# Seven block products in place of eight in the last tile of a windowed attention with a GELU MLP behind it

## The chip, the core and the metric

The kernel runs on one core of a Trainium2 chip. A core has five engines with a queue of instructions each: TensorE (PE in the profile; its weight loads are shown as PEld), VectorE (DVE), ScalarE (ACT), GpSimd (POOL) and SyncE (SP), which here issues the DMAs. They meet through semaphores. Matmuls write to PSUM, which this kernel uses as eight banks of 128 partitions by 512 f32; everything else lies in SBUF. The metric is the device time of the program in microseconds (us): lower is better.

## The reference

Eight batches of eight heads, 576 positions of 64 numbers. Attention looks back over a window of 128 positions with a linear bias, and its output, 4608 tokens of 512 numbers, goes through an MLP of 2048 features.

```python
scores = scale * np.matmul(q, k.transpose(0, 1, 3, 2))
mask = (rel >= 0) & (rel < window)
scores = np.where(mask, scores + bias[None], -1000000000.0)
attn = np.exp(scores - max); attn = attn / (attn.sum + 1e-09)
x = (attn @ v) as (4608, 512)
h = x @ w_in                                      # (512, 2048)
g = 0.5 * h * (1.0 + erf(h * inv_sqrt2))
return (g @ w_out).astype(np.float32)             # (2048, 512)
```

## The kernel before

The 4608 tokens are nine tiles of 512 (`TT`), the batches eight of 576. While tile t goes through the MLP, the attention of batch t + 1 runs between its steps, so the last two tiles (t = 7 and 8) have no attention beside them. Everything is f32 in effect: each operand is kept as two f16 halves, a high and a low one, with powers of two as scales, and a product is three matmuls (high by high, low by high, high by low).

For a tile, `mlp_in` (line 588) makes 16 blocks of 128 features: 4 chunks of the 512 inputs by 3 terms, 12 matmuls (line 595) of 128x128 weights (`wi`, a piece of 256 features each) by 512 tokens, into one PSUM bank of the four with the tag "mm". ACT evicts it with gelu into an f32 buffer `g32` (line 618, three of them, tag "ob"), POOL makes the high half (619), and DVE the low half through the helper `low_part` (146). `mlp_out` (line 638 on) then makes 4 blocks of 128 tokens by 512 outputs, 48 matmuls (653) each, with the features as weights; DVE and ACT evict in turn (663, 661), and SP writes the block to memory (664). So a tile is 192 + 192 matmuls of 512 columns.

In the start-up the weights arrive as int64 words holding doubles. `weights_in` turns two pieces at a time to f32 (`to_float32`), takes the largest exponent of each, and splits them (ACT high, DVE low). `stat_v`, `split_v` and `split_qk` do the same for a batch's attention operands; their buffers `qbuf`, `kbuf`, `vbuf` and `e_main` lie idle once the last batch is done.

Each engine's order is not the order of the code: the framework's scheduler sets it when the kernel is built, from its own estimates and priorities (`tc.high_priority`). Pools with a tag and a count of buffers make an instruction wait until the buffer's earlier readers are done.

Of the kernel before, what the change touches and what calls it, by code (L numbers as in the profile page):

```python
# [10 lines left out]
F16 = mybir.dt.float16  # L11
F32 = mybir.dt.float32
# [8 lines left out]
P = 128  # L21
# [34 lines left out]
def attention_gelu_mlp(  # L56
# [9 lines left out]
):  # L66
    nc = tc.nc
    pool = ctx.enter_context(tc.tile_pool(name="sb", bufs=1))
    psum = ctx.enter_context(tc.tile_pool(name="ps", bufs=1, space=bass.MemoryType.PSUM))

    def small(shape, name, bufs, tag=None, dt=F32):
# [64 lines left out]
        inverse(sc, pw)  # L136
        return pw, sc

    def inverse(sc, pw):

        nc.vector.tensor_scalar(
            sc.bitcast(I32), pw.bitcast(I32), -1.0, float((127 + 127 + 13) << 23), op0=ALU.mult, op1=ALU.add
        )

    def low_part(dst, src, scale, high):
# [105 lines left out]
    def weights_out_scale():  # L251


        over_partitions(stwo, NWP, True, STAT_FLOOR)
        pow2_of_words(pwo, stwo)
        nc.vector.tensor_tensor(out=pwo, in0=pwo, in1=pww, op=ALU.mult)
        most = pool.tile([P, 1], F32, name="most")
        nc.vector.tensor_reduce(out=most, in_=pwo, axis=AX.X, op=ALU.max)
        nc.vector.tensor_scalar_max(most, most, FLOOR)
        pwm = pool.tile([P, 1], F32, name="pwm")  # L260
        nc.vector.tensor_scalar(pwm.bitcast(I32), most.bitcast(I32), EXPMASK, None, op0=ALU.bitwise_and)
        k2 = pool.tile([P, 1], F32, name="k2")
        inverse(k2, pwm)
# [44 lines left out]
    def stat_v(b, gate=None):  # L308


        stat = small([P, 1], f"stv{b}", 2, tag="stv")
        if gate is not None:
            nc.vector.tensor_copy(stat, gate)
        absmax(stat, v32s[b].rearrange("p h n d -> p (h n d)"))
        pwv[b], scv[b] = pow2(f"v{b}", stat, 1, 3, b < 2)
        if b == 0:
            pwx[b], sx[b] = pwv[b], scv[b]
        else:
            pwx[b] = small([P, 1], f"pwx{b}", 3, tag="pwx")
            nc.vector.tensor_tensor(out=pwx[b], in0=pwv[b - 1], in1=pwv[b], op=ALU.max)  # L320
            sx[b] = small([P, 1], f"sx{b}", 3, tag="sx")
            inverse(sx[b], pwx[b])
# [265 lines left out]
    def mlp_in(t, fc):  # L588
        n, k = divmod(fc, 2)
        ph = psum.tile([P, TT], F32, tag="mm", name=f"h{t}_{fc}", bufs=4)  # L590
        x = x_tile(t)
        i = 0
        for cc in range(NCC):
            for a, b in ((0, 0), (1, 0), (0, 1)):
                nc.tensor.matmul(  # L595
                    ph, wi[n][:, a, cc, k * P : (k + 1) * P], x[:, cc, b, :],
                    start=(i == 0), stop=(i == 3 * NCC - 1),
                )
                i += 1
        q, r = divmod(fc, 4)  # L600
        if r == 0:
            if t == 0:
                g_of[t, q] = pool.tile([P, 4, TT], F32, tag="g", name=f"g{t}_{q}", bufs=4)
            else:
                g_of[t, q] = pool.tile([P, 4, 2, TT], F16, tag="g", name=f"g{t}_{q}", bufs=4)
        g = g_of[t, q]
        if t == 0:
            nc.scalar.activation(g[:, r, 0:WHOLE], ph[:, 0:WHOLE], AF.Gelu, scale=gsc[t, n])
            if k == 0:
                rests[n] = pool.tile([P, 2, TT - WHOLE], F32, tag="ob", name=f"g32_{t}_{n}", bufs=3)  # L610
            rest = rests[n][:, k]
            nc.scalar.activation(rest, ph[:, WHOLE:TT], AF.Gelu, scale=gsc[t, n])
# [5 lines left out]
        nc.scalar.activation(g32, ph, AF.Gelu, scale=gsc[t, n])  # L618
        nc.gpsimd.tensor_scalar(g[:, r, 0], g32, gsg[t, n], 1.0, op0=ALU.mult, op1=ALU.mult)  # L619
        low_part(g[:, r, 1], g32, gsg[t, n], g[:, r, 0])  # L620

    def halves_of(g, r):
# [8 lines left out]

    def out_scale(t):
        so[t] = small([P, 1], f"so{t}", 2, tag="so")
        nc.vector.tensor_scalar(so[t], pwm, pwx[t], 2.0 ** -17, op0=ALU.mult, op1=ALU.mult)

    o_ps = {}

    def mlp_out(t, tb, fc, first=0, last=NFC - 1):
# [18 lines left out]
        if fc == last:  # L657
            ob = pool.tile([P, DM], F32, tag="ob", name=f"ob{t}_{tb}", bufs=3)
            so_t = 1.0 if whole else so[t]
            if tb % 2:  # L660
                nc.scalar.activation(ob, o, AF.Copy, scale=so_t)  # L661
            else:
                nc.vector.tensor_scalar_mul(ob, o, so_t)  # L663
            nc.sync.dma_start(out[t * TT + tb * P : t * TT + (tb + 1) * P, :], ob)


    units = {}
# [52 lines left out]
    for n in range(NWP):  # L720
        if n == 2:
            load_qk(1)
        with tc.high_priority(400):
            for k in range(2):
                mlp_in(0, 2 * n + k)
        weights_out_raw(n)
        if n == 7:
            stat_v(1, low_of_first(8))
            split_qk(1, low_of_first(5))
            split_v(1)  # L730
            load_v(2)
        fetch(1)
# [71 lines left out]


# [34 lines left out]
```

## Time and profile before

| | us |
|---|---|
| three runs | 949.90, 952.62, 952.87 (median 952.62) |
| profiled execution | 956.14, its span 954.3 |
| PE, DVE, ACT, POOL busy in the span | 920.4, 626.1, 493.4, 214.5 |
| next to last tile's matmuls begin | 784.62 |
| last tile's first matmul to the end of the span | 867.5 to 954.3 |

A row of groups reads: line, engine, operation, output <- inputs, partitions x elements and type, count | busy us, mean ns of one | idle time of the engine before them and what ended it. A row of the timeline begins with start and length. A PE row's ends are modelled and overlap, so lengths of single matmuls do not add up; the step from start to start does.

### The profile page before, as it was taken

Reading aid. Unit: us, or ns where it says so; the run is one execution under the profiler, and the core shown is the slowest. Engines: PE = TensorE matmul, PEld = TensorE weight load, DVE = VectorE, ACT = ScalarE, POOL = GpSimd, SP = SyncE. Lnnn points to the kernel's source line nnn. Section 1 sums busy time; section 2 is a strip of 40 time slices with the busy share of each in tenths; the row PEclk is TensorE's granted clock in tenths of the full one; section 3 lists DMA queues with packets and bytes.
Section 4 is the critical chain, followed back from the end, with each engine's and each line's share of the span. In section 5 each row is a group of like instructions: output and inputs, shape, how many; then the busy total and the mean of one; then the engine's idle time right before and its main releaser. Section 6 shows DMA issues by size and latency. Waiting matters only on the chain.

```text
span 954.3 us, 17680 instructions
## 1 busy us (share of the span) xinstructions
PE 920.4 (96%) x7068; PEld 448.8 (47%) x7068; DVE 626.1 (66%) x1270; ACT 493.4 (52%) x1071; POOL 214.5 (22%) x444
## 2 busy tenths in 40 slices
PE   7979999889999899999999999999999999999998
PEld 3554444544544444444544454444544454444443
DVE  6799989689786877497768876777566722201200
ACT  5978967767653664366525653564366313101200
POOL 1010000023001542053314430353044312201200
PEclk9889999799999999999999999999999999999999
DMA  9517433961473226522472346144312430000000
GB/s 313 211 65 264 179 105 94 208 191 29 98 176 99 50 58 144 148 46 55 77 201 46 56 94 178 52 77 94 73 30 50 92 75 1 1 23 23 1 12 33
DMA packets 172450, 91.18 MB, mean 96 GB/s; under 512 B 132560, under 2 KB 153168, under 8 KB 172240
## 3 DMA queue, kind: packets, MB, share of 16 engines
q1 hardware_dynamic: 172368, 90.06, 37.7%
q8 instruction: 55, 0.90, 0.4%
q14 instruction: 27, 0.22, 0.1%
HBM read 46.53 MB, written 9.44 MB: 59 GB/s over the span
## 4 chain that ended last, share of the span: by engine, by line
PE 54%; DMA 2%; DVE 2%; ACT 2%; issue 1%; SPq 0%; POOL 0%; DVEq 0%
PE o L653 26%; PE h L595 22%; PE av L554 3%; PE sc L410 2%; DMA v<-vp 1%; DMA q<-qp 1%; DVE stv L214 1%; DMA et<-e_main 1%; ACT vbuf L332 1%; DVE vbuf L146 0%; ACT s L505 0%; DVE kbuf L146 0%; ACT L618 0%; ACT L505 0%; SPq L305 0%
## 5 line engine op out<-in xcount | busy, mean ns | idle before, releaser
L595 PE MATMUL h<-x,wi 128*128 128x512 f16 x1728 | 385.0, 381 | 6.6 <-ACT g L618 3.0
L653 PE MATMUL o<-wo,g 128*128 128x512 f16 x1224 | 276.4, 379 | 0.2 <-DVE wo L146 0.2
L595 PEld LDWEIGHTS <-wi 128*128 128x128 f16 x1728 | 166.8, 98 | 209.2 <-issue 12.3
L653 PEld LDWEIGHTS <-g 128*128 128x128 f16 x1632 | 155.0, 98 | 186.6 <-issue 2.3
L146 DVE SCALAR_TENSOR_TENSOR g<-g,sg,g 128x512 f16<-128x512 f32 (+1 forms) x144 | 114.1, 805 | 92.7 <-POOL g L619 91.5
L619 POOL TENSOR_SCALAR g<-g,sg 128x512 f16<-128x512 f32 x128 | 100.4, 788 | 316.7 <-ACT g L618 312.4
L505 ACT ACTIVATE s<-s,nmax 128x192 f32<-128x192 f32 x252 | 111.2, 442 | 103.2 <-DVE nmax L502 103.0
L618 ACT ACTIVATE g<-h,gs 128x512 f32<-128x512 f32 x128 | 85.9, 687 | 135.8 <-PE h L595 111.0
L146 DVE SCALAR_TENSOR_TENSOR e_main<-s,z,e_main 128x192 f16<-128x192 f32 x252 | 107.3, 468 | 15.0 <-POOL e_main L514 10.2
L514 POOL TENSOR_SCALAR e_main<-s,z 128x192 f16<-128x192 f32 x180 | 87.1, 503 | 84.9 <-ACT s L505 29.3
L653 PE MATMUL o<-wo_first,g 128*128 128x512 f16 x408 | 94.6, 382 | 2.8 <-DMA wo_first<-wo 2.8
L410 PE MATMUL sc<-kbuf,qbuf 64*64 64x192 f16 (+1 forms) x1656 | 75.6, 264 | 10.8 <-DMA kbuf<-kp 4.5
L432 DVE SCALAR_TENSOR_TENSOR s<-sc,cs,bias_h 128x384 f32<-128x384 f32 x112 | 63.7, 606 | 14.3 <-PE sc L410 14.1
L567 ACT ACTIVATE x<-av,cx 128x448 f16<-128x448 f32 (+6 forms) x52 | 23.7, 474 | 72.8 <-PE av L554 72.6
L437 POOL MEMSET s<- 64x128 f32 (+1 forms) x112 | 19.2, 172 | 185.8 <-DVE s L432 167.3
L502 DVE TENSOR_REDUCE nmax<-s 128x5 f32<-128x960 f32 (+1 forms) x56 | 58.4, 1044 | 2.1
L661 ACT ACTIVATE ob<-o,so 128x512 f32<-128x512 f32 x17 | 11.5, 678 | 91.2 <-PE o L653 91.1
L410 PEld LDWEIGHTS <-qbuf 64*64 64x64 f16 x1512 | 36.1, 106 | 43.0 <-issue 40.2
L663 DVE TENSOR_SCALAR ob<-o,so 128x512 f32<-128x512 f32 x17 | 12.6, 744 | 60.0 <-PE o L653 60.0
L554 PEld LDWEIGHTS <-vbuf 128*64 128x64 f16 x1680 | 43.3, 115 | 12.4 <-issue 11.5
L554 PE MATMUL av<-et,vbuf 128*64 128x128 f16 (+1 forms) x1680 | 46.4, 216 | 2.6 <-DMA et<-e_main 2.6
L505 ACT ACTIVATION_READ_ACCUMULATOR s<-s,nmax 128x1 f32 x252 | 47.1, 187 | 0.0
(139 smaller groups left out, 737.8 us busy)
## 6 DMA issues: line engine op xcount, KB each, us to landing
v<-vp SPq DMA_DIRECT2D x32, 320.0 KB, 5.1
out<-ob SPq DMA_DIRECT2D x36, 256.0 KB, 2.1
raw<-w_in SPq DMA_DIRECT2D x8, 1024.0 KB, 14.2
raw<-w_out SPq DMA_DIRECT2D x8, 1024.0 KB, 5.3
q<-qp SPq DMA_DIRECT2D x7, 1152.0 KB, 6.2
k<-kp SPq DMA_DIRECT2D x7, 1152.0 KB, 7.1
qbuf<-qp SPq DMA_DIRECT2D x4, 288.0 KB, 5.1
kbuf<-kp SPq DMA_DIRECT2D x4, 288.0 KB, 5.5
```

Source lines behind the costliest of these rows:

```text
L146: nc.vector.scalar_tensor_tensor(out=dst, in0=src, scalar=scale, in1=high, op0=ALU.mult, op1=ALU.subtract)
L410: nc.tensor.matmul(ps[bank][o, n, 0:W], a, m, start=(i == 0), stop=(i == len(terms) - 1 and b > 0), skip_group_check=True,)
L432: nc.vector.scalar_tensor_tensor(out=s[:, bank[0] : bank[0] + k, :], in0=ps[bank][:, 0:k, 0:W], scalar=cs, in1=bias.broadcast_to([P, k, W] ...
L502: nc.vector.tensor_reduce(out=nmax[:, r], in_=s[:, r], axis=AX.X, op=ALU.max, negate=True)
L505: nc.scalar.activation(s[:, i, :], s[:, i, :], AF.Exp, bias=nmax[:, i : i + 1], accum_out=z[:, i : i + 1])
L514: nc.gpsimd.tensor_scalar(e[:, i, 0, c], s[:, i], z[:, i : i + 1], 1.0, op0=ALU.mult, op1=ALU.mult)
L554: nc.tensor.matmul(av[r, (j - blocks[0]) * QB : (j - blocks[0] + len(js)) * QB], v32s[b][:, hp, kb, r] if b < EXACT else vbuf[:, vi, hp, k ...
L567: nc.scalar.activation(x[:, 0], av[:, :n], AF.Copy, scale=c)
L595: nc.tensor.matmul(ph, wi[n][:, a, cc, k * P : (k + 1) * P], x[:, cc, b, :], start=(i == 0), stop=(i == 3 * NCC - 1),)
L618: nc.scalar.activation(g32, ph, AF.Gelu, scale=gsc[t, n])
L619: nc.gpsimd.tensor_scalar(g[:, r, 0], g32, gsg[t, n], 1.0, op0=ALU.mult, op1=ALU.mult)
L653: nc.tensor.matmul(o, both[:, a, c], wo[n][:, b, k, :], start=(fc == first and i == 0), stop=(fc == last and i == 2),)
```

## The change

For the last tile (t = 8, `FAST`) both products are done by blocks. Tokens, inputs and features are each halved, so that a product of two matrices is one of 2x2 blocks, and Winograd's form of Strassen's scheme takes seven block products in place of eight, with sums of blocks on both sides. The class `Seven` does it for a group of 512 features (four groups, `d`): seven times 12 matmuls of 128x128 weights by 256 tokens, in two PSUM banks, `u` and `v`. Some products are added in the bank on what stands there (p1, then p6, p7, p4 in `u`; p5, then p3 in `v`), with the value copied out by ACT in between. DVE makes the sums, ACT the gelu and the high halves, DVE the low ones. The features' own sums for the second product (`sum`) are made there too. The second product (`add` in `seven_all`) has seven parts of 48 matmuls of 256 columns, in banks named u, v, x, y and z.

Sums of weights are made on DVE from the halves of `wi` and `wo` (`sums_of_weights`, `sums_of_weights_out`), ACT and DVE split them. Those of `wi` go through DRAM (`stored`); a quarter of them comes back in place over `wi` when the next to last tile's first product is done, and three quarters stream through three small rooms, 256 KB at a time. Those of `wo` stay in `qbuf`, `kbuf`, `vbuf` and `e_main`. Sixteen such parts are placed behind tile 6's code and beside the steps of tile 7 (`PARTS_AT`), two sums of x at its end. In tile 7 ACT makes the high halves in place of POOL. Two pieces of `wi` now share one scale, exponents of the scales leave a bit more room, and the first two pieces' matmuls in tile 0 lose their higher priority.

```diff
@@ weights_in
-        pow2_of_words(pww[:, r], stat)
-        inverse(sww[:, r], pww[:, r])
+        nc.vector.tensor_tensor(out=stat[:, 0:1], in0=stat[:, 0:1], in1=stat[:, 1:2], op=ALU.max)
+        pow2_of_words(pww[:, r], stat[:, 0:1].broadcast_to([P, len(ns)]))
+        inverse(sww[:, r], pww[:, r], 12)
@@ mlp_in
-        nc.gpsimd.tensor_scalar(g[:, r, 0], g32, gsg[t, n], 1.0, op0=ALU.mult, op1=ALU.mult)
+        if t + 1 < FAST:
+            nc.gpsimd.tensor_scalar(g[:, r, 0], g32, gsg[t, n], 1.0, op0=ALU.mult, op1=ALU.mult)
+        else:
+            nc.scalar.activation(g[:, r, 0], g32, AF.Copy, scale=gsg[t, n])
@@ new
+    def sums_of_blocks(name, blocks, order, gate=None):
...
+        for m, b in enumerate(blocks):
+            nc.vector.tensor_tensor(
+                out=r[:, 2 * m : 2 * m + 2], in0=b[0], in1=b[1], op=ALU.add
+            )
+        b11, b12, b21, b22 = (r[:, n] for n in order)
+        nc.vector.tensor_tensor(out=b11, in0=b12, in1=b11, op=ALU.subtract)
+        nc.vector.tensor_tensor(out=b12, in0=b22, in1=b12, op=ALU.subtract)
+        nc.vector.tensor_tensor(out=b22, in0=b22, in1=b11, op=ALU.subtract)
+        nc.vector.tensor_tensor(out=b21, in0=b21, in1=b22, op=ALU.subtract)
+        return r
+
+    def halves_of_sums(dst, r):
+        nc.scalar.copy(dst[0], r)
+        nc.vector.tensor_tensor(out=dst[1], in0=r, in1=dst[0], op=ALU.subtract)
+
+    def sums_of_weights(d, i, gate=None):
...
+        halves_of_sums([st[:, a] for a in range(2)], r)
+        for n, k in ((T1, 0), (T2, 3), (T3, 2), (T4, 1)):
+            nc.sync.dma_start(stored[n, d, :, :, i], st[:, :, k])
...
+    class Seven:
...
+        def add(self, ps, w, m, first):
+            n = 0
+            for k in range(2):
+                for i in range(2):
+                    for a, b in ((0, 0), (1, 0), (0, 1)):
+                        nc.tensor.matmul(
+                            ps[:, k * HT : (k + 1) * HT], w(a, i)[:, k * P : (k + 1) * P], m(b, i),
+                            start=first and n == 0, stop=True, skip_group_check=True,
+                        )
+                        n += 1
...
+        def p7(self):
+            self.add(self.u, lambda a, i: streams[T3][:, a, i], lambda b, i: sums[i][:, b, S3], False)
+            s3 = self.s3 = self.room("s3")
+            nc.scalar.copy(s3, self.u)
+            nc.vector.tensor_tensor(out=s3, in0=self.v, in1=s3, op=ALU.add)
+            self.out(1, 1, s3)
+
+        def p4(self):
+            self.add(self.u, lambda a, i: streams[T4][:, a, i], lambda b, i: self.x[:, 2 * i + 1, b, HT:TT], False)
+            s4 = rooms[3 * (self.d % 2) + 2]
+            self.out(0, 1, self.u, s4)
+            self.sum(S1, self.s3, s4, self.s3, ALU.add)
+            self.sum(S3, s4, self.s1, s4, ALU.subtract)
+            self.sum(S2, self.s1, self.s3, self.s1, ALU.subtract)
...
+        for d in every:
+            q[d].p1()
+            q[d].p2()
+            if d:
+                q[d - 1].p4()
+                stream(T4, d)
+            q[d].p6()
...
@@ main loop
-        with tc.high_priority(400):
+        with tc.high_priority(400 if n >= 2 else 0):
...
+    PARTS_AT, SUMS_AT = (1, 3, 6, 9, 12, 15, 17, 19, 21, 23, 25, 27), (28, 29)
...
+        if t == FAST:
+            seven_all(t)
+            break
```

What this makes of the engines' orders is shown at three places.

DVE beside the next to last tile's first product, before: the low halves of its features (`g`), one behind the other.

```order
L146 SCALAR_TENSOR_TENSOR g_0_9596<-g_7_1_9614,sg_0_9579,g_0_9596 128x512
L146 SCALAR_TENSOR_TENSOR g_0_9596<-g_7_2_9631,sg_0_9579,g_0_9596 128x512
L146 SCALAR_TENSOR_TENSOR g_0_9596<-g_7_3_9648,sg_0_9579,g_0_9596 128x512
L146 SCALAR_TENSOR_TENSOR g_1_9665<-g_7_4_9666,sg_0_9579,g_1_9665 128x512
L146 SCALAR_TENSOR_TENSOR g_1_9665<-g_7_5_9683,sg_0_9579,g_1_9665 128x512
```

Now (`ti` is a block of sums of weights, `r` one of x; the low halves are on line 149):

```order
L149 SCALAR_TENSOR_TENSOR g_0_9665<-g_7_2_9714,sg_0_9648,g_0_9665 128x512
L712 TENSOR_TENSOR ti_0_9801<-wi_770 128x512
L712 TENSOR_TENSOR ti_0_9801<-wi_773 128x512
L761 TENSOR_TENSOR r_1_10252<-r_1_10252 128x256
L716 TENSOR_TENSOR ti_1_9735<-ti_1_9735 128x256
L149 SCALAR_TENSOR_TENSOR g_0_9665<-g_7_3_9731,sg_0_9648,g_0_9665 128x512
L716 TENSOR_TENSOR ti_0_9801<-ti_0_9801 128x256
L762 TENSOR_TENSOR r_1_10252<-r_1_10252 128x256
L717 TENSOR_TENSOR ti_1_9735<-ti_1_9735 128x256
L149 SCALAR_TENSOR_TENSOR g_1_9665<-g_7_4_9763,sg_0_9648,g_1_9665 128x512
```

Two to four passes over sums now stand between two low halves, and two blocks of sums (ti_0 and ti_1) take turns.

PE in the last tile, before, where the first product begins behind the tile before it:

```order
L653 MATMUL o_3_10015<-wo_1679,g_3_9803 128x512
L653 LDWEIGHTS g_3_9803
L653 MATMUL o_3_10015<-wo_1679,g_3_9803 128x512
L595 LDWEIGHTS wi_679
L595 MATMUL h_0_10073<-x_8835,wi_679 128x512 [waits DVE_49]
```

Now, between the last matmul of p7 of group 1 (u_1) and the first of p1 of group 2 (u_2); x_out is a bank of the second product, and g_0 are features of group 0:

```order
L789 MATMUL u_1_10378<-room_9586,room_9587 128x256
L901 LDWEIGHTS g_0_10298 [waits Activation_49]
L901 MATMUL x_out<-qbuf,g_0_10298 128x256 [waits PE_49]
L901 LDWEIGHTS g_0_10298
L901 MATMUL x_out<-qbuf,g_0_10298 128x256
L901 LDWEIGHTS g_0_10298 [waits DVE_49]
L901 MATMUL x_out<-qbuf,g_0_10298 128x256
L789 LDWEIGHTS wi_741
L789 MATMUL u_2_10496<-x_8844,wi_741 128x256 [waits Activation_49]
```

Matmuls of the second product have moved in between the block products of the first.

DVE in the start-up, before, where the low halves of weights 2 and 3 (wi_707, wi_710) are made:

```order
L146 SCALAR_TENSOR_TENSOR wi_707<-zi_686,sww,wi_707 128x1024
L196 SCALAR_TENSOR_TENSOR zi_714<-raw_127,zi_714 128x1024
L476 TENSOR_SCALAR vbuf<-s_3_444,z_3_543 128x192 x5
L146 SCALAR_TENSOR_TENSOR wi_710<-zi_686,sww,wi_710 128x1024
L192 TENSOR_SCALAR zi_742,stw_741<-zi_742 128x1024
L196 SCALAR_TENSOR_TENSOR zi_714<-raw_129,zi_714 128x1024
```

Now (they are named wi_712 and wi_715):

```order
L199 SCALAR_TENSOR_TENSOR zi_719<-raw_130,zi_719 128x1024
L481 TENSOR_SCALAR vbuf<-s_3_447,z_3_546 128x192 x5
L195 TENSOR_SCALAR zi_748,stw_747<-zi_748 128x1024
L199 SCALAR_TENSOR_TENSOR zi_719<-raw_132,zi_719 128x1024
L587 TENSOR_SCALAR sg_2_710<-sww,scv_316 128x2
L240 TENSOR_TENSOR stw_718<-stw_718 128x1
L195 TENSOR_SCALAR zi_748,stw_747<-zi_748 128x1024
L149 SCALAR_TENSOR_TENSOR wi_712<-zi_690,sww,wi_712 128x1024
L149 SCALAR_TENSOR_TENSOR wi_715<-zi_690,sww,wi_715 128x1024
```

Both low halves have moved behind the next pieces' conversion, and a maximum of two columns (`stw`, line 240) has come in.

More of the change, by code (lines that the diff above doesn't have):

```diff
@@ L321, in stat_v @@
             sx[b] = small([P, 1], f"sx{b}", 3, tag="sx")
-            inverse(sx[b], pwx[b])
+            inverse(sx[b], pwx[b], 12 if b >= FAST else 13)
         for t in (b - 1, b):
@@ L664, in mlp_out @@
             nc.sync.dma_start(out[t * TT + tb * P : t * TT + (tb + 1) * P, :], ob)
+    stored = dram.tile([4, NWP // 2, P, 2, 2, 256], F16, name="stored")
+    S2, S3, S4, S1 = range(4)
+    T2, T3, T4, T1 = range(4)
+    sums, streams, rooms, slots = [], [], [], []
+    sums_out = [e.rearrange(p)[:, 0 : 8 * 512].rearrange("p (a k s f) -> p a k s f", a=2, k=2, s=4)
+                for e, p in ((qbuf, "p a s -> p (a s)"), (kbuf, "p a s -> p (a s)"),
+                             (vbuf, "p a h n d -> p (a h n d)"), (e_main, "p g a k -> p (g a k)"))]
@@ new lines, in sums_of_x @@
+    def sums_of_x(t, i):
+        x = x_tile(t)[:, 2 * i : 2 * i + 2]
+        r = pool.tile([P, 2, TT], F32, tag="v32", name=f"r{t}_{i}", bufs=1)
+        nc.vector.tensor_tensor(out=r, in0=x[:, :, 0], in1=x[:, :, 1], op=ALU.add)
+        a11, a21, a12, a22 = r[:, 0, 0:HT], r[:, 0, HT:TT], r[:, 1, 0:HT], r[:, 1, HT:TT]
+        nc.vector.tensor_tensor(out=a22, in0=a21, in1=a22, op=ALU.add)
+        nc.vector.tensor_tensor(out=a21, in0=a11, in1=a21, op=ALU.subtract)
+        nc.vector.tensor_tensor(out=a11, in0=a22, in1=a11, op=ALU.subtract)
+        nc.vector.tensor_tensor(out=a12, in0=a12, in1=a11, op=ALU.subtract)
+        flat = r.rearrange("p c n -> p (c n)")
+        hi, lo = (sums[i][:, a].rearrange("p s f -> p (s f)") for a in range(2))
+        nc.scalar.copy(hi, flat)
+        nc.vector.tensor_tensor(out=lo, in0=flat, in1=hi, op=ALU.subtract)
@@ new lines, in stream_next, with seven_all, add, features @@
+    def stream_next(t, n, d):
+        if d < NWP // 2 - 1:
+            stream(n, d + 1)
+    def seven_all(t):
+        room_for_features()
+        q = [Seven(t, d) for d in range(NWP // 2)]
+        last, every = len(q) - 1, range(len(q))
+        for d in every:
[5 more added lines that the diff above has]
+            q[d].p6()
+            if d < last:
+                stream(T2, d + 1)
+            if d:
+                q[d - 1].p3()
+            q[d].p5()
+            q[d].p7()
+            if d < last:
+                stream(T3, d + 1)
+        ps = {}
+        def add(name, f, w, ds, tbs=range(2)):
+            first = name not in ps
+            if first:
+                tag = "mm" if name in ("u", "v") else "att"
+                ps[name] = psum.tile([P, 2, DM // 2], F32, tag=tag, name=f"{name}_out", bufs=4)
+            for tb in tbs:
+                for d in ds:
+                    for k in range(2):
+                        for a, b in ((0, 0), (0, 1), (1, 0)):
+                            nc.tensor.matmul(
+                                ps[name][:, tb], f(d, a)[:, k, tb * P : (tb + 1) * P], w(d, b, k),
+                                start=first, stop=True, skip_group_check=True,
+                            )
+                            first = False
+        def features(hi, tok):
+            return lambda d, a: g_of[t, d][:, 2 * hi : 2 * hi + 2, a, tok * HT : (tok + 1) * HT]
+        def weights(hi, half):
+            return lambda d, b, k: wo[2 * d + hi][:, b, k, half * (DM // 2) : (half + 1) * (DM // 2)]
+        def sum_of_features(s):
+            return lambda d, a: q[d].place(s, a)
+        def sum_of_weights(n):
+            k_of = (T1, T3, T4, T2).index(n)
+            return lambda d, b, k: sums_out[d][:, b, k, k_of]
+        def copy(name):
+            c = rooms[len(copies)].rearrange("p (b f) -> p b f", b=2)
+            copies.append(c)
+            nc.scalar.activation(c, ps[name], AF.Copy, scale=so[t])
+            return c
+        def plus(dst, name, c, tb=slice(0, 2)):
+            nc.vector.scalar_tensor_tensor(
+                out=dst[:, tb], in0=ps[name][:, tb], scalar=so[t], in1=c[:, tb], op0=ALU.mult, op1=ALU.add
+            )
+        def leave(name, c, tok, half, tbs=(slice(0, 2),)):
+            ob = pool.tile([P, 2, DM // 2], F32, tag="ob", name=f"ob{t}_{tok}_{half}", bufs=3)
+            rows = out[t * TT + tok * HT : t * TT + (tok + 1) * HT, half * (DM // 2) : (half + 1) * (DM // 2)]
+            rows = rows.rearrange("(b p) f -> p b f", p=P)
+            for tb in tbs:
+                plus(ob, name, c, tb)
+                nc.sync.dma_start(rows[:, tb], ob[:, tb])
+        copies = []
+        one, two = (features(0, 0), weights(0, 0)), (features(1, 0), weights(1, 0))
+        add("u", *one, every[:last])
+        q[last].p4()
+        add("u", *one, every[last:])
+        c1 = copy("u")
+        q[last].p3()
+        add("x", features(1, 1), sum_of_weights(T4), every)
+        add("v", *two, every)
+        leave("v", c1, 0, 0)
+        add("u", sum_of_features(S2), sum_of_weights(T2), every)
+        c2 = copy("u")
+        add("y", sum_of_features(S1), sum_of_weights(T1), every)
+        add("u", sum_of_features(S3), sum_of_weights(T3), every)
+        plus(c2, "y", c2)
+        c3 = copy("u")
+        leave("x", c3, 1, 0)
+        leave("y", c3, 1, 1)
+        add("z", sum_of_features(S4), weights(1, 1), every)
+        leave("z", c2, 0, 1, [slice(0, 1), slice(1, 2)])
@@ L779, in attention_gelu_mlp @@
                     mlp_out(t, tb, fc)
+            if t + 1 == FAST:
+                if step in PARTS_AT:
+                    parts.pop(0)()
+                if step == NFC:
+                    sums_in_place()
+                if step in SUMS_AT:
+                    sums_of_x(FAST, SUMS_AT.index(step))
             if b >= B:
@@ L803, in attention_gelu_mlp @@
                 split_qk(b + 1)
+        if t + 2 == FAST:
+            room_for_sums()
+            for n in range(4):
+                parts.pop(0)(gate=unit(b, NPAIR - 1).z[:, NG - 1 : NG] if n < 2 else None)
 def kernel(q, k, v, moe_w_in, moe_w_out):
```

106 lines of the change are left out of this document (99 added, 7 removed).

## The prediction

> **What bounds the kernel now.** I read the page's busy line and its 40 slices first, then a table of busy time by stage, then the last tile's groups and its timeline.
>
> ```profile
> PE 920.4 (96%) x7068; PEld 448.8 (47%) x7068; DVE 626.1 (66%) x1270; ACT 493.4 (52%) x1071; POOL 214.5 (22%) x444
> PE   7979999889999899999999999999999999999998
> DVE  6799989689786877497768876777566722201200
> ACT  5978967767653664366525653564366313101200
> 60.00:114.00 54.00, 51.84 (x292) 26.52 (x293) 52.25 (x90) 46.80 (x78) 1.08 (x3) 0.97 0.65 224
> 114.00:216.00 102.00, 92.03 (x786) 47.34 (x785) 88.38 (x180) 73.16 (x161) 9.87 (x25) 0.95 0.56 140
> 784.60:867.40 82.80, 82.80 (x385) 37.55 (x384) 13.74 (x19) 13.65 (x19) 11.20 (x16) 1.00 0.04 13
> 867.40:954.30 86.90, 83.15 (x386) 37.49 (x383) 13.52 (x18) 13.06 (x19) 11.12 (x16) 1.00 0.04 16
> ```
>
> The columns of a stage are its length, then busy us and counts of PE, PEld, DVE, ACT and POOL, then the granted clock. In the next to last tile (784.6 to 867.4) and in the last one PE never rests and the clock is 1.00, while DVE and ACT do some 14 us of work in 83. These are the two tiles that the change touches: PE is the bound, and two engines have 69 us each to give. In the start-up (60 to 216) DVE is as full as PE, and there a new order can hurt.
>
> ```profile
> L595 PE MATMUL h<-x,wi 128*128 128x512 f16 x192 | 41.6, 379 | 0.0
> L595 PEld LDWEIGHTS <-wi 128*128 128x128 f16 x192 | 18.8, 98 | 22.6
> L146 DVE SCALAR_TENSOR_TENSOR g<-g,sg,g 128x512 f16<-128x512 f32 x16 | 12.0, 751 | 41.3 <-POOL g L619 41.3
> L618 ACT ACTIVATE g<-h,gs 128x512 f32<-128x512 f32 x16 | 11.0, 687 | 30.4 <-PE h L595 30.4
> 940.02 2.75 PE L653 MATMUL o<-wo_first,g 128*128 128x512 f16 x12
> 942.61 7.93 PE L653 MATMUL o<-wo,g 128*128 128x512 f16 x36
> 950.59 0.69 ACT L661 ACTIVATE ob<-o,so 128x512 f32<-128x512 f32 x1 [20.03 <-PE o L653]
> 951.30 0.33 SPq L664 DMA_DIRECT2D out<-ob  x1
> ```
>
> Matmuls overlap: the mean of one is 379 ns, but 36 of them last 7.93 us from the first start to the last end, so the step is (7.93 - 0.38) / 35 = 0.2157 us for 512 columns. The last tile is 384 of them, 82.8 us, and then 3.7 us of tail: an eviction of 0.69 us on ACT and a transfer that lands at 954.3.
>
> **PE in the last tile.** Now 2 products x 4 groups of 512 features x 7 block products x 12 matmuls = 672 matmuls of 256 columns; eight block products would be 768. No 256-column matmul stands in the trace; the nearest rows are short ones with a fresh 128x128 weight load each:
>
> ```profile
> 18.67 0.20 PE L422 MATMUL sc<-adders 128*128 128x64 bf16 x1
> 18.71 0.25 PE L422 MATMUL sc<-bias_h,adders 128*128 128x192 bf16 x1
> 18.79 0.19 PE L422 MATMUL sc<-adders 128*128 128x64 bf16 x1
> ```
>
> 64 columns step to the next in 0.04 us and 192 columns in 0.08 us. So a full weight load fits behind 64 columns, and 256 columns lie between 0.08 and 0.2157: on a straight line of the 192 and the 512 they cost 0.08 + 64/320 x 0.136 = 0.107, and half of 0.2157 is 0.108. I take 0.109, with 0.107 and 0.113 as ends (the rows are rounded to 10 ns). 672 x 0.109 = **73.2 us, 9.6 us less**; the ends are 71.9 and 75.9.
>
> [...]
>
> **ACT and DVE in the last tile.** For each group of 512 features ACT now does 14 passes of 512 columns (copies out of PSUM, gelu, high halves) and DVE 14 (sums, low halves): 56 each, beside 28 x 1.31 = 36.7 us of first-product matmuls.
>
> ```profile
> 54.13 1.45 ACT L493 COPY et<-tp 128x512 f32<-128x512 f32 x3
> 57.94 2.19 ACT L204 ACTIVATE wi<-zi,sww 128x1024 f16<-128x1024 f32 x2 [2.36 <-DVE sww L141]
> 65.65 1.28 DVE L146 SCALAR_TENSOR_TENSOR wi<-zi,sww,wi 128x1024 f16<-128x1024 f32 x1
> 66.85 1.21 DVE L192 TENSOR_SCALAR_CACHE_REDUCE zi<-zi 128x1024 f32<-128x1024 f32 x1
> 70.33 0.75 DVE L146 SCALAR_TENSOR_TENSOR x<-av,scv,x 128x512 f16<-128x512 f32 x1
> 70.99 1.22 DVE L193 SCALAR_TENSOR_TENSOR zi<-zi,raw 128x1024 int32<-128x1024 int32 x1
> 129.50 0.87 DVE L146 SCALAR_TENSOR_TENSOR g<-g,sg,g 128x256 f16<-128x256 f32 x2
> ```
>
> Back to back, DVE steps 0.66 us for 512 elements (70.33 to 70.99), 1.20 for 1024 and 0.39 for 256 (0.87 less one of 0.48); when each waits for the one before it is the full 0.75, 1.28 and 0.48. Plain adds of two tensors have no large row; I price them as these. [...] So DVE needs 56 x 0.66 = 37 to 56 x 0.75 = 42 us, and ACT about the same. That is more than 36.7, but the order puts 33 second-product matmuls between the block products and 48 ahead of the last two, 8.8 us, so that the part ends at 45.4 us. I walked its rows, engine by engine, with 1.31 us for 12 matmuls, full durations where a row waits for another, and 0.2 us from the end of the last matmul's step to its reader (950.59 above against 942.61 + 36 x 0.2157). Every PE wait came out met, with 1 to 3 us to spare: the second use of an accumulator stands two to four block products (2.7 to 5 us) behind its first, and the copy between them ends about 1 to 2 us after the first. The last low half of the features is due at about 51 us and made at about 48. I book **0** for these waits, 0 to 2 as range.
>
> Weights that are read back from DRAM come 256 KB at a time into the room of the ones before:
>
> ```profile
> out<-ob SPq DMA_DIRECT2D x36, 256.0 KB, 2.1
> v<-vp SPq DMA_DIRECT2D x32, 320.0 KB, 5.1
> ```
>
> The tightest is the first: its room is free at 5.5 us of the tile and it is read at 9.2. With 2.1 it is in time, with 5.1 PE waits 1.9 us; I take the former (nearly the same size, little traffic) and keep 1.9 within the range above. SP has nothing else to issue then.
>
> **The next to last tile.** DVE gets 14 us more of everything: behind the first gelu and up to the low half of the 16th, 11 passes of 1024, 30 of 512 (16 of them low halves) and 28 of 256. That is 11 x 1.20 + 30 x 0.66 + 28 x 0.39 = 43.9 us at the steps, 50.0 at the full durations.
>
> ```profile
> 768.29 0.75 DVE L146 SCALAR_TENSOR_TENSOR x<-av,cxl,x 128x512 f16<-128x512 f32 x1 [0.20 <-ACT x L567]
> 781.19 0.28 DVE L146 SCALAR_TENSOR_TENSOR x<-av,cx,x 128x64 f16<-128x64 f32 x1 [7.58 <-ACT x L567]
> 784.62 15.70 PE L595 MATMUL h<-x,wi 128*128 128x512 f16 x72
> 826.06 2.75 PE L653 MATMUL o<-wo_first,g 128*128 128x512 f16 x12
> ```
>
> Ahead of these stand the first sums of weights and of x, begun between the last softmaxes. 3 x 0.75 + 3 x 0.48 = 3.7 us of them push the pass of 768.29 to 772; then come 9 x 0.48 + 2 x 1.28 + 5 x 0.75 = 10.6 us, the low half of x that ran at 781.19 (now near 783), and 8 x 0.48 + 3 x 0.75 + 1.28 = 7.4 us, to 790.5. The 43.9 us from there end at 834.4. The last low half is needed by the 48th matmul of the first output row, 826.2 + 47 x 0.2157 = 836.3. At the steps it is 2 us early, at the full durations 4.2 us late. The dependent 256-column steps come from two blocks in turn, so most wait for nothing, and I take the steps, plus **0.5 us** for what doesn't interleave. The tile's first product needs the low half of x at 784.62 + 8 x 0.2157 = 786.3: in time at 783. On ACT the high halves move in from POOL: 32 x 0.69 + 10 x 1.1 = 33 us of 41. Gelu lags PE by up to 3 us; four PSUM banks allow 7.
>
> **The start-up.** Low halves of weights 2 and 3 move behind three or four passes of 1.2 us, from 62 and 65.7 to some 69.5.
>
> ```profile
> 73.06 8.79 PE L595 MATMUL h<-x,wi 128*128 128x512 f16 x40
> 82.97 31.24 PE L595 MATMUL h<-x,wi 128*128 128x512 f16 x144 [1.11 <-ACT g L612]
> 136.39 2.82 DVE L214 TENSOR_REDUCE stv<-v 128x1 f32<-128x2560 f32 x1 [2.51 <-DMA v<-vp]
> 170.46 0.59 PE L653 MATMUL o<-wo_first,g 128*128 128x512 f16 x1 [2.77 <-DMA wo_first<-wo]
> ```
>
> They are first used behind 48 matmuls, at about 83, so nothing waits. Eight early matmuls and 26 of attention swap places: 0. Later the reduction of v (waiting for its DMA to 136.39) moves ahead of the scale of the output weights, which costs their split about 1.5 us, and the last low half of them moves ahead of a reduction of 1.15; against that, output matmuls are pulled into PE's waits. In 114 to 216 PE idles 102.0 - 92.0 = 10 us in all. I book **0**, and -3 to +3 as ends.
>
> **The tail.** The last eviction is 256 columns on DVE (0.48 for 0.69), and the last transfer half as large: **-0.3 us**, between -0.6 and 0.
>
> **Sum.** The profiled execution took 956.14 us, 1.84 more than its span. 956.14 - 9.6 + 0.5 - 0.3 = 946.7. It lay 3.5 us above the median of the three runs (952.62); the same terms on the median give 952.62 - 9.4 = **943.2 us**.
>
> **Rivals.** (1) DVE runs at full durations in the next to last tile, or the start-up's order loses 3 us: 943.2 + 2.5 to 6 = 945.7 to 949.3. For it: 50 us of work against 45.8 of room. Against: the two-block interleaving. (2) The start-up gains 2 to 4 us, its waits being filled: 939 to 941. [...] (4) **Slower:** hand-offs in the last tile's first product. A sum on DVE, its high half on ACT and its low half on DVE follow each other, and both queues are in order, so each of DVE's 56 passes could pay for a wait. PE's first part ends at 45.4 us by the walk; DVE starts at 2.9. The gain of 9.4 is gone when DVE takes 45.4 + 9.4 - 2.9 = 51.9 us, 0.93 a pass; at 1.1 it takes 61.6, and the kernel is at 943.2 + 19.1 = 962. The trace has 0.75 where POOL is out of the way, as it will be.
>
> **Chances.** Forecast 0.62 (940 to 945.5), (1) 0.20, (2) 0.06, (3) 0.05, (4) 0.07. About 0.3% (2.9 us) can be told from no change: faster, below 949.8, has the forecast, (2), and nearly all of (1), 0.86; within, the rest of (1) and the milder half of (3) and (4), 0.07; slower 0.07. The range 939.5 to 949.5 leaves out (3), (4) and the edge of (2).
>
> **What would show it.** Right: 672 matmuls of 256 columns stepping at 0.107 to 0.113, the last tile 73 to 75 us long with no PE wait over 1 us, DVE and ACT 35 to 45 us busy in its first half. Wrong: PE waiting for DVE at the end of the next to last tile's first output row (1), for ACT or DVE between block products (4), steps over 0.113 (3), or the last tile starting more than 3 us off 867.4 (start-up).

## The result and the profile after

The changed kernel takes **943.8 us** (median of 7 runs, 941.6 to 947.4) against 952.6 for the kernel before (7 runs): a ratio of 0.991, 95% interval 0.989 to 0.994. The profiled execution is the slowest of its seven, 947.36 us with a span of 945.3, as that of the kernel before (956.14) lay above all of its own.

The page's busy line and slices, then the table of busy time by stage: next to last tile's two products, the last tile in two parts, and the tail (columns as in the prediction).

```profile
PE 909.2 (96%) x7356; PEld 475.2 (50%) x7356; DVE 720.3 (76%) x1445; ACT 546.5 (58%) x1146; POOL 194.2 (21%) x412
PE   6969999789999899999999999999999999999998
DVE  6798989779876877678767877787656799991771
785.14:826.60 41.46, 41.46 (x194) 18.79 (x193) 41.17 (x73) 29.99 (x40) 0.00 (x0) 1.00 0.43 128
826.60:868.04 41.44, 41.44 (x194) 18.81 (x193) 24.70 (x43) 9.02 (x10) 0.00 (x0) 1.00 0.07 26
868.04:904.40 36.36, 36.36 (x335) 32.58 (x334) 23.86 (x37) 26.10 (x43) 0.00 (x0) 1.00 0.26 74
904.40:941.56 37.16, 37.16 (x341) 33.08 (x338) 16.05 (x24) 11.69 (x19) 0.00 (x0) 1.00 0.07 22
941.56:945.30 3.74, 0.00 (x0) 0.00 (x0) 0.88 (x2) 0.00 (x0) 0.00 (x0) 1.00 0.21 70
```

PE is as full as before in both tiles and waits for nothing from 785 to its last matmul; DVE's last eight slices, 22201200 before, are 99991771. In the first product of the next to last tile DVE works 41.17 of 41.46 us. The last tile is 73.52 us from its first matmul to the end of its last, where it was 83.05. Its first rows of PE, and the group of weight loads that goes with them:

```profile
868.04 1.47 PE L789 MATMUL u<-x,wi 128*128 128x256 f16 x12
869.35 1.47 PE L789 MATMUL v<-x,wi 128*128 128x256 f16 x12
L789 PEld LDWEIGHTS <-wi 128*128 128x128 f16 x192 | 18.8, 98 | 2.4
```

Twelve matmuls of 256 columns step on in 1.31 us, so one takes 0.109, with a weight load of 98 ns for each.

Runs of one kernel differ by up to 9 us, but not there. In the profiles of the eleven kernels below that have the changed start-up (all but before and e8), tile 7 begins anywhere between 778.5 and 785.2, and what follows is equal to 0.1 us wherever nothing was edited, but for the tail of the old ending: 3.78, 4.13 and 3.80 in before, e5 and e6. So experiments are read first from three stages of each trace, and from the times second:

| kernel | time, us | tile 7 (first matmul to tile 8's first) | last tile (to PE's end) | tail (to the span's end) |
|---|---|---|---|---|
| before | 952.6 | 82.88 | 83.05 | 3.78 |
| after | 943.8 | 82.88 | 73.52 | 3.71 |
| e1 first block product twice | 949.4 | 82.88 | **78.76** | 3.71 |
| e2 low halves twice, last tile | 946.4 | 82.88 | **76.23** | **5.63** |
| e3 low halves twice, tile 7 | 943.4 | 82.88 | 73.52 | 3.72 |
| e4 low halves three times, tile 7 | 948.9 | **88.94** | 73.52 | 3.72 |
| e5 preparation alone | 952.9 | 82.88 | 83.05 | 4.13 |
| e6 first product alone | 947.7 | 82.88 | 78.29 | 3.80 |
| e7 POOL's high halves in tile 7 | 947.3 | **85.01** | 73.52 | 3.72 |
| e8 old priority in tile 0 | 945.3 | 82.88 | 73.52 | 3.72 |
| e9 last eviction whole | 942.7 | 82.88 | 73.52 | **4.03** |
| e10 POOL busy in the last tile | 947.0 | 82.88 | **77.25** | 3.73 |
| e11 two banks at the end | 944.2 | 82.88 | 73.52 | **3.22** |

### The profile page after: what moved, and what is told of

Same layout as the page of the kernel before. It is cut to its first block, busy times and chain, and to the rows that moved or that the text cites. A ratio compares the mean times of both kernels' runs of the same rounds, so it can differ in the third digit from the quotient of the medians.

```text
span 945.3 us, 18563 instructions
## 1 busy us (share of the span) xinstructions
PE 909.2 (96%) x7356; PEld 475.2 (50%) x7356; DVE 720.3 (76%) x1445; ACT 546.5 (58%) x1146; POOL 194.2 (21%) x412
## 4 chain that ended last, share of the span: by engine, by line
PE 68%; DVE 7%; ACT 5%; DMA 4%; issue 2%; SPq 1%; DVEq 0%; ACTq 0%
PE o L661 31%; PE h L600 22%; PE av L559 4%; PE sc L415 4%; DMA v<-vp 2%; PE u L789 2%; PE u_out L901 2%; PE v L789 2%; DMA et<-e_main 1%; ACT s L510 1%; DVE stv L217 1%; DVE vbuf L149 1%; DVE nmax L507 1%; ACT L623 1%; ACT vbuf L337 1%
## 5 line engine op out<-in xcount | busy, mean ns | idle before, releaser
L600 PE MATMUL h<-x,wi 128*128 128x512 f16 x1536 | 344.7, 382 | 6.5 <-ACT g L623 3.0
L661 PE MATMUL o<-wo,g 128*128 128x512 f16 x1080 | 244.7, 379 | 1.1 <-DVE wo L149 1.1
L600 PEld LDWEIGHTS <-wi 128*128 128x128 f16 x1536 | 148.2, 98 | 188.0 <-issue 14.2
L661 PEld LDWEIGHTS <-g 128*128 128x128 f16 x1440 | 136.0, 98 | 164.6 <-issue 3.0
L623 ACT ACTIVATE g<-h,gs 128x512 f32<-128x512 f32 x112 | 74.8, 685 | 81.0 <-PE h L600 57.4
L149 DVE SCALAR_TENSOR_TENSOR g<-g,sg,g 128x512 f16<-128x512 f32 (+1 forms) x128 | 101.9, 811 | 22.6 <-POOL g L625 19.4
L625 POOL TENSOR_SCALAR g<-g,sg 128x512 f16<-128x512 f32 x96 | 78.5, 823 | 193.4 <-ACT g L623 189.6
L661 PE MATMUL o<-wo_first,g 128*128 128x512 f16 x360 | 83.2, 380 | 0.3 <-DMA wo_first<-wo 0.3
```

The costliest lines, as they stand in the source:

```text
L149: nc.vector.scalar_tensor_tensor(out=dst, in0=src, scalar=scale, in1=high, op0=ALU.mult, op1=ALU.subtract)
L600: nc.tensor.matmul(ph, wi[n][:, a, cc, k * P : (k + 1) * P], x[:, cc, b, :], start=(i == 0), stop=(i == 3 * NCC - 1),)
L661: nc.tensor.matmul(o, both[:, a, c], wo[n][:, b, k, :], start=(fc == first and i == 0), stop=(fc == last and i == 2),)
```

## The experiments

Theory: PE's columns are the whole of the gain, and all that was added for them is hidden, with a few us of room. Rivals: hand-offs in the last tile, DVE late in tile 7, the start-up.

**Is it PE's columns?** Three kernels ask for that.

```diff
+            self.add(self.u, lambda a, i: self.lo[:, a, 2 * i], ...)      # e1: p1's matmuls again
```

> The first of the seven block products is made twice in each of the four groups of the last tile (48 more matmuls of 256 columns, same output). If TensorE alone sets the last tile: 48 x 0.109 = 5.2 us more than the changed kernel's 943.8, so 949.0, and a last tile of 78.5 us. If hand-offs to ACT and DVE set it, the extra matmuls fall into waits: 943.8 to 945. If weight loads were exposed anywhere: more than 5.2.

Measured: 949.4 us, ratio to before 0.9968 (0.9953 to 0.9983), and a last tile of 78.76, 5.24 more than after. 48 x 0.109 is 5.23: none of the added matmuls fell into a wait, as the theory had it.

```diff
-            seven_all(t); break                          # e5: the plain last tile
-            nc.sync.dma_start(wi[2 * d + 1][:, :, 0 : NCC : 2], stored[T1, d])
+            nc.sync.dma_start(streams[d % 3], stored[T1, d])
```

> All of the change but its use: the sums are made, stored and read back (the quarter that went over the weights goes to a streaming room), scales, priorities and ACT's high halves are as in the changed kernel, and the last tile is made by eight block products as before, 384 matmuls of 512 columns. Theory: the preparation costs what the profiles differ by at the last tile's first matmul, +0.5 us over the kernel before: 953.1 beside its 952.6, a ratio of 1.0005, and the last tile is 82.8 us long. Rival: the preparation or the new start-up gains or loses some us that the last tile's gain hides or pads: a ratio under 0.998 or over 1.003.

Measured: 952.9 us, ratio 1.0009 (0.9991 to 1.0027); the last tile is 83.05 again. So the preparation costs nothing that can be measured: the interval is -0.9 to +2.6 us. The features' own sums are not in this kernel.

```diff
-            if hi < tok: return                          # e6: all four blocks of features,
-            self.sum(...)                                #     and no sums of them
-        add("u", *one, ...) ... leave("z", ...)
+        for tb in range(NTB):
+            for fc in range(NFC):
+                mlp_out(t, tb, fc)
```

> Only the first product of the last tile by seven block products; the second is made of 192 matmuls of 512 columns, and the features' own sums are left out. Theory: each product brings half of the 9.6 us, so 36.6 + 41.4 = 78.0 us for the last tile, 948.6 in all, 4.8 over the changed kernel. Rival (the first product is paid back in hand-offs that the second product's matmuls cover): over 950.

Measured: 947.7 us, ratio 0.9961 (0.9941 to 0.9981); last tile 78.29 where 78.0 was expected (the plain second product accumulates in the banks that attention no longer uses, an edit not shown above). Each product brings its half, 4.8 us, without help from the other.

**How much room has DVE in tile 7?** The kernel after, DVE's timeline (start, length) where the sixteenth low half is made, in the middle of sums of output weights (`to`):

```profile
829.19 1.22 DVE L724 TENSOR_TENSOR kbuf<-to,kbuf 128x1024 f16<-128x1024 f32 x1
830.32 1.28 DVE L712 TENSOR_TENSOR to<-wo 128x512 f32<-128x512 f16 x2
831.53 0.74 DVE L149 SCALAR_TENSOR_TENSOR g<-g,sg,g 128x512 f16<-128x512 f32 x1
832.19 1.28 DVE L712 TENSOR_TENSOR to<-wo 128x512 f32<-128x512 f16 x2
```

It is done at 832.3. Its reader is the 48th matmul of the first output row, 826.6 + 47 x 0.2157 = 836.7: 4.5 us of room. The next two kernels make each of the 16 low halves of tile 7 twice and three times.

```diff
         low_part(g[:, r, 1], g32, gsg[t, n], g[:, r, 0])
+        for _ in range(1 if t == FAST - 1 else 0):           # e3; 2 for e4
+            low_part(g[:, r, 1], g32, gsg[t, n], g[:, r, 0])
```

> Each of the 16 low halves of features in the next to last tile is made twice (10.6 us more of DVE). The scheduler moves some sums of weights behind the last of them, so that 44.1 us of passes stand from the first low half to the sixteenth, where 39.7 stood: 4.4 more. The trace of the changed kernel has the sixteenth low half 4.5 us ahead of its need. Theory: 0 to +0.5 us over 943.8. Rival (DVE was just on time, as its 99% busy says): +4 us, 948.

> The same low halves three times (21.1 us more of DVE). Here 57.4 us of passes stand ahead of the sixteenth low half, 17.6 more than in the changed kernel. Theory: 17.6 - 4.5 of room = +13 us over 943.8, so 957, with PE waiting for DVE at the features ahead of or in the first output row of the next to last tile. Rival (the sums for the last tile are what is late, not the low halves): PE's waits stand in the last tile instead. If DVE has no bearing: 0.

Measured for e3: 943.4 us, ratio 0.9902 (0.9881 to 0.9923), tile 7 unchanged. Its last pass of a low half and two PE rows at the end of the first output row:

```profile
829.28 0.75 DVE L149 SCALAR_TENSOR_TENSOR g<-g,sg,g 128x512 f16<-128x512 f32 x1
830.43 2.54 PE L663 MATMUL o<-wo_first,g 128*128 128x512 f16 x11
832.80 0.38 PE L663 MATMUL o<-wo,g 128*128 128x512 f16 x1
```

The pass ends at 830.03. In the old order the 48th matmul would stand at 820.28 + 47 x 0.2157 = 830.42, so even there it would have been in time, by 0.4 us. But the scheduler put 11 matmuls of the next row ahead of it, and it starts at 832.80. So the room was real, but this kernel, with 2.8 us left, doesn't show where it ends.

Measured for e4: 948.9 us, ratio 0.9967 (0.9952 to 0.9983), tile 7 6.1 us longer. The theory asked for 13, and for waits at the low halves; it missed both. PE's waits of e4 in the last two tiles (us in total, times, longest):

```profile
PE h L600 <- ACT g L623: 3.2, 3, 2.0
PE o L663 <- ACT g L623: 0.5, 1, 0.5
```

and two of its stretches, around the longest wait and behind it:

```profile
802.70:813.60 10.90, 8.55 (x40) 3.72 (x38) 10.90 (x19) 7.86 (x11) 0.00 (x0) 1.00 0.12 36
813.60:817.30 3.70, 3.70 (x11) 1.35 (x10) 3.70 (x6) 1.82 (x3) 0.00 (x0) 0.54 0.60 175
```

No wait is for the low halves' reader. The scheduler, which knew of the extra passes, put the 48th matmul behind 94 others in place of 47, which is worth 47 x 0.2157 = 10.1 us of the 13. What bites instead stands ahead of it: gelu waits for one of three f32 buffers that a late low half still reads (ACT's waits for DVE's low halves come to 10.2 us there), and PE waits for gelu, 3.7 us in all. This idle time counts from the modelled end of the matmul before; from start to start the four steps are 4.3 us longer than 0.2157. And behind the longest of these waits the granted clock is 0.54 for 3.7 us: the 24 matmuls from 813.42 on last 7.03 us, (7.03 - 0.38) / 23 = 0.289 a step in place of 0.2157, 1.7 us more in all. 4.3 + 1.7 is the 6.1 but for 0.1. PE was idle for 2.0 us just ahead of it; that this wait is what lowered the clock isn't shown.

**Does it matter that ACT took the high halves from POOL in tile 7?**

```diff
-        if t + 1 < FAST:
+        if t < FAST:                                     # e7
             nc.gpsimd.tensor_scalar(g[:, r, 0], g32, gsg[t, n], 1.0, op0=ALU.mult, op1=ALU.mult)
```

> POOL makes the high halves in the next to last tile, as before the change. PE's order is unchanged. Theory: the low halves wait one more hand-off and DVE's passes may get dearer beside POOL (0.75 us for one in the profile before); 68 passes stand ahead of the sixteenth low half, with 4.5 us of room: 0 to +1 us over 943.8. Rival (the move to ACT is what lets DVE keep up): +2 to +6.

Measured: 947.3 us, ratio 0.9945 (0.9925 to 0.9964), tile 7 2.1 us longer, so the rival's low end. POOL's group in e7 (busy, mean ns of one), and PE's waits:

```profile
L625 POOL TENSOR_SCALAR g<-g,sg 128x512 f16<-128x512 f32 x16 | 25.1, 1576 | 43.2 <-ACT g L623 43.0
```

```profile
PE o L661 <- POOL g L625: 1.2, 1, 1.2
PE o L661 <- DVE g L149: 0.6, 1, 0.6
```

DVE's timeline in e7, a little ahead of these waits:

```profile
821.41 1.09 DVE L712 TENSOR_TENSOR to<-wo 128x512 f32<-128x512 f16 x1
822.43 0.41 DVE L716 TENSOR_TENSOR to<-to 128x256 f32<-128x256 f32 x1
822.76 1.09 DVE L149 SCALAR_TENSOR_TENSOR g<-g,sg,g 128x512 f16<-128x512 f32 x1
```

POOL's passes, 0.70 us each in this place of the kernel before, take 1.58 on average beside a full DVE. Of DVE's passes of 512, six of the 16 low halves and seven of the 18 sums go from 0.75 and 0.68 to 1.09 or more; the others keep their length, as do the passes of 1024. PE then waits for the last high half and for its low half.

**What do hand-offs in the last tile cost?** First with a schedule that knows of the extra work, then with one that doesn't.

```diff
             low_part(dst[1], v, sg, dst[0])
+            low_part(dst[1], v, sg, dst[0])              # e2
```

> Every low half that DVE makes in the last tile is made twice: 28 more passes of 512, 18.5 us at a step of 0.66, so DVE has 58 us of work in place of 40 in a tile of 73. The scheduler places more matmuls of the second product between the block products. Theory (DVE is cover as long as its work ends before the last parts of the second product need it): 0 to +2 us over 943.8. Rival (the hand-offs of the first product set the end, as in the prediction's slower case, 2.9 + 58 against 45.4): about +16, 960.

```diff
+                if d == 0:                               # e10: x of tile 7, which nothing reads any more
+                    nc.gpsimd.tensor_copy(old[:, 0:1], g_of[t, 0][:, 0, 0, 0:1])
+                    for m in range(36):
+                        nc.gpsimd.tensor_scalar(b, a, 1.0, 1.0, op0=ALU.mult, op1=ALU.mult)
```

> POOL gets 36 passes of 512 f32 over a buffer that nothing reads any more, in a chain that begins with the first features of the last tile; the orders of TensorE, DVE and ACT stay as they are. Beside POOL a DVE pass of 512 took 1.09 us in place of 0.75 in the run with POOL's high halves. Theory (the prediction's slower case, with its sum): DVE starts 2.9 us into the tile and makes 56 passes, TensorE's first part ends at 45.4; at 0.93 a pass +9.6 us, at 1.09 +18.5, so a time of 953 to 962 with TensorE waiting between block products. Rival (with twice the low halves the cost was only 2.7 us in the last tile, so DVE has room): 0 to +3, 944 to 947. If POOL doesn't slow DVE here, 0.

Busy time summed over the last tile, of the kernel after, of e2 and of e10:

```profile
sum 73.52, PE 73.52 PEld 65.66 DVE 39.91 ACT 37.79 POOL 0.00; mean PE 24.51 PEld 21.89 DVE 13.30 ACT 12.60 POOL 0.00
```

```profile
sum 76.23, PE 74.34 PEld 65.53 DVE 56.25 ACT 38.44 POOL 0.00; mean PE 24.78 PEld 21.84 DVE 18.75 ACT 12.81 POOL 0.00
```

```profile
sum 77.25, PE 74.02 PEld 65.56 DVE 46.20 ACT 38.20 POOL 30.89; mean PE 24.67 PEld 21.85 DVE 15.40 ACT 12.73 POOL 10.30
```

PE's waits of e10 there, and a piece of its DVE timeline ahead of the longest:

```profile
PE z_out L907 <- ACT g L808: 2.0, 1, 2.0
PE v L789 <- DVE room_s L831: 0.8, 1, 0.8
PE u L789 <- ACT room_s L826: 0.5, 1, 0.5
```

```profile
889.41 1.09 DVE L819 TENSOR_TENSOR room_s<-room_s 128x512 f32<-128x512 f32 x1
890.42 0.68 DVE L831 TENSOR_TENSOR room_s<-v,room_s 128x512 f32<-128x512 f32 x1
891.02 0.74 DVE L149 SCALAR_TENSOR_TENSOR slots<-s,sg,slots 128x512 f16<-128x512 f32 x1
891.68 1.09 DVE L819 TENSOR_TENSOR room_s<-s,room_s 128x512 f32<-128x512 f32 x1
```

In e2 DVE works 16.3 us more and PE's last tile is 2.7 longer; the time is 946.4, ratio 0.9943 (0.9924 to 0.9963). The scheduler had moved more second-product matmuls between the block products, and also 48 of them nearly to the end (u_out, with five of z behind them), so that a copy on ACT and four evictions stand behind PE in place of two: 1.9 us of tail. By the stages that is 4.6 in all, above the theory's 2 and far below the rival's 16. In e10 only 6.3 us more of DVE, in the same order, cost 3.7; the time is 947.0, ratio 0.9953 (0.9934 to 0.9973). The theory's numbers don't hold for e10: the mean pass came to 0.77 us, not 0.93 or more, since POOL was busy for 31 us only and a pass that reads PSUM (line 831) stayed at 0.68; and the rival's 0 to +3 is just passed, with 3.2 by the times and 3.7 by the tile. What stands is that PE waits between block products: with a fixed order, a sixth more of DVE's work is enough for that.

**The start-up and the tail.**

```diff
-        with tc.high_priority(400 if n >= 2 else 0):
+        with tc.high_priority(400):                      # e8
```

> All matmuls of tile 0's first product have the higher priority again, as before the change. Theory: the 0.5 us by which the last two tiles start later in the changed kernel go or stay: -0.5 to +0.5 us against 943.8. Rival (the lower priority of the first two pieces is worth something in the start-up): +1 to +3; or it costs: -1 to -3.

Measured: 945.3 us, ratio 0.9928 (0.9905 to 0.9951), which the times can't tell from the changed kernel. In its one profile PE waits once for 5.59 us in tile 0 (ahead of 90.70, for ACT's `g`), and tile 7 begins at 787.0, later than in any other; but kernels with one and the same start-up lie 6.7 us apart there, so this decides nothing.

```diff
-        leave("z", c2, 0, 1, [slice(0, 1), slice(1, 2)])
+        leave("z", c2, 0, 1)                             # e9
```

> The last part of the output leaves in one eviction of 2x256 columns and one transfer of 256 KB in place of two halves. From TensorE's end to the end of the span the trace has 3.8 us before the change and 3.7 after it, where the prediction had 0.3 less. If the halves are worth something and were paid elsewhere: 4.0 to 4.3 here. If a transfer's fixed time sets the tail, whatever its size: 3.7 to 3.8, but for the eviction, 0.3 longer than half of it.

Measured: a tail of 4.03 (time 942.7, ratio 0.9910, 0.9877 to 0.9942). By this one profile the two halves are worth 0.3 us over one whole, about what the tail of the old ending varies by; over the kernel before, whose whole eviction on ACT has 3.78, they are worth hardly anything. The end of the kernel after shows why; the PE row is z's matmuls, then both halves of its eviction:

```profile
938.78 0.82 PE L901 MATMUL z_out<-wo_first,g 128*128 128x256 f16 x6
939.43 2.13 PE L901 MATMUL z_out<-wo,g 128*128 128x256 f16 x18
941.60 0.88 DVE L928 SCALAR_TENSOR_TENSOR ob<-z_out,so,room_s 128x256 f32<-128x256 f32 x2 [2.13 <-PE z_out L901]
```

Both halves begin behind PE's last matmul, though the first half's own 24 matmuls were done 2 us earlier: they share a tile in one bank. So 0.88 us of evictions stand at the end, not 0.48. Hence one more kernel:

```diff
-        add("z", sum_of_features(S4), weights(1, 1), every)
+        for tb, name in enumerate(("z", "zz")):          # e11: a bank for each half
+            add(name, sum_of_features(S4), weights(1, 1), every, [tb])
```

> The last part of the output is accumulated in two banks of PSUM, one for each 128 tokens, in place of one. In the changed kernel both halves of its eviction begin 0.04 us behind the last matmul, though the first half's matmuls end 2.1 us earlier. If the shared bank is why the tail did not get its 0.3 us: the first eviction moves ahead of TensorE's end, one of 0.44 is left behind it, and the tail is 3.7 - 0.4 = 3.3 us. Rival (the wait stays, or the transfer's fixed time covers it): 3.7. The time, 943.4 to 943.8, can't tell the two apart; the trace can.

Its timeline at the same place:

```profile
937.49 2.13 PE L901 MATMUL zz_out<-wo,g 128*128 128x256 f16 x18
937.88 0.47 DVE L928 SCALAR_TENSOR_TENSOR ob<-z_out,so,room_s 128x256 f32<-128x256 f32 x1
939.66 0.48 DVE L928 SCALAR_TENSOR_TENSOR ob<-zz_out,so,room_s 128x256 f32<-128x256 f32 x1 [1.30 <-PE zz_out L901]
```

The first half now leaves beside PE, and the tail is 3.22, 0.5 less: as the theory had it. A second bank is also a second tile to the framework that sets the waits, so which of the two held the first half back is not shown. The time, 944.2 (ratio 0.9908, 0.9889 to 0.9927), can't show so little; no kernel here is measurably faster than the changed one.

## Why the prediction was right, point by point

**PE in the last tile, -9.6: right.** 83.05 became 73.52, 9.53 less, and 672 matmuls step at 0.109. Rival (3), steps over 0.113 because weight loads show (chance 0.05), did not come: loads of 98 ns are busy for 32.58 of 36.36 us, behind matmuls that step at 109 ns. Had each been exposed in full, 672 x 0.098 = 66 us would stand on top; no run shows any of it. The row of 0.04 us that the prediction leaned on was thin evidence, three matmuls in a burst; the 672 in a stream are what shows it. e1 (+5.24 for 48) and e6 (half the gain for half the change) show that nothing else is in it.

**Waits in the last tile, 0: right**, and the first part ended at 45.5 us of the tile as walked (the last matmuls of `v` end at 913.56), with 45.4 predicted. DVE is busy for 39.9 us in the tile and ACT for 37.8, as priced (37 to 42); the sign "35 to 45 us busy in its first half" is narrowly missed, with 31.9 and 33.0 up to 913.56, the end of the first part. But the price of the slower case was too kind. Its sum let DVE run without a pause until 45.4 us. By it e10's 43.2 us of passes (46.2 less four evictions of 0.75) would have cost 2.9 + 43.2 - 45.4 = 0.7; they cost 3.7. DVE itself pauses for ACT in between (5.9 us ahead of low halves of `g` in the changed kernel), which the sum leaves out; that this is the whole reason isn't shown. If it goes on one for one, the gain would be gone at some 49 us of DVE, an estimate from this one point, and not at 51.9.

**Streamed weights, 0: right.** Nine loads of 256 KB are issued from 873.69 on; with the three ahead of them the median is 2.7 us to landing, between the 2.1 and 5.1 of the prediction, and no matmul waits for one.

**The next to last tile, +0.5: the mechanism right, the size not.** DVE's low half of x (784.3, needed at 786.9) and the sixteenth low half came in time, the latter 4.5 us early where 2 were predicted, and tile 7 is 82.88 us long before and after: the 0.5 booked for it did not come. Mis-sized was the price of a plain sum: I took the steps of SCALAR_TENSOR_TENSOR, 0.66 for 512 and 0.39 for 256; TENSOR_TENSOR steps at 0.60 (830.32 to 831.53 for two), 0.335 and, for 1024, 1.14. By these the 68 passes there, one of 1024 fewer than the prediction counted, are 39.7 us in place of its 43.9. The line on ACT's high halves gave room in PSUM as the point; e7 says that the move is worth 2.1 us for another reason, POOL's and DVE's passes side by side.

**The start-up, 0 (-3 to +3): inside its range, but hardly 0.** Tile 8 begins 0.54 us later in the one profile than in the other, and e5 has 0.8 us for the start-up and all other preparation, within its interval of nothing. More runs say a bit more. Take from every run's span the lengths of its last three stages in the table, as if they were the same in each run: then tile 7 begins at 780.6 us on average in 77 runs of the kernel before and at 781.6 in 96 of the eleven kernels with the changed start-up. By this estimate the start-up costs 1.0 us, give or take 0.6 (0.7 by the medians). Which of its changes does it stays open.

**The tail, -0.3: wrong, -0.07.** The step that failed is "the last eviction is 256 columns on DVE (0.48 for 0.69)": two such evictions, 0.88 us, stand behind the last matmul. What follows them is 2.79 us where it was 3.05, but the old ending varies by more than that. e11 shows the mechanism: with a bank for each the 0.5 us come.

**Sum.** For the profiled run 956.14 - 9.53 + 0.54 - 0.07, and 0.2 more outside the span (947.36 against 945.3), is 947.3; it took 947.36, and 946.7 was predicted. By the medians 943.2 was forecast and 943.8 measured. That the two are so near is in part luck. The last tile's 9.5 is right by its mechanism, but the small terms missed on both sides: 0.5 booked for tile 7 that did not come, 0.2 too much gained at the tail, nothing for the start-up, and nothing for the 0.3 us more that runs of the changed kernel spend outside their span (2.1 against 1.8).

## What to carry to other kernels

Seven block products for eight brought 9.5 of the 10.4 us that an eighth of the tile is, in a stage where TensorE is the bound and two other engines idle: here a matmul of 256 columns still hides its own weight load (98 ns in a step of 109), and steps a little above half of one of 512 (0.109 against 0.108). The sums have to fit somewhere: here they fill DVE in the tile ahead to 41.17 of 41.46 us, and no run tries a second tile. Price each kind of pass by its own rows, and look for the few us of room that each hand-off has: 16.3 us more of DVE that the scheduler knew of cost 4.6 (e2), 6.3 that it didn't know of cost 3.7 (e10). Read small effects from stages of the trace: but for the old ending they repeat to 0.1 us, where whole runs differ by 9.

## What the runs showed of the hardware

Unexpected were three things. Beside POOL many DVE passes of 512 with two operands in SBUF take 1.09 us or more in place of 0.68 (a sum) or 0.75 (a low half), 13 of 34 in e7, while the eight that read PSUM beside POOL in e10 stay at 0.67 to 0.69; POOL's own take 1.58 on average beside a full DVE (e7), 0.70 in the same place of the kernel before. Why some passes beside POOL are slowed and others not isn't shown. A PE wait of 2.0 us was once followed by 3.7 us at a clock of 0.54 (e4), while around another of 2.0 us the clock stayed at 1.00 (e10). And TENSOR_TENSOR follows itself every 0.60 us for 512 elements, though each is shown as 0.68 long (the kernel after, 830.32 to 831.53 for two).
